# Score matmuls that read 32 rows of keys and queries a head instead of 17

## The chip, the cores and the metric

The kernel runs on one core of a Trainium2 chip, in one launch. The metric is the device time of that core in microseconds; lower is better. A core has a matrix engine (TensorE, in the profile PE for its matmuls and PEld for its weight loads), a vector engine (VectorE, DVE), an engine for functions such as exp and tanh (ScalarE, ACT), a general one (GpSimd, POOL), and queues for transfers to and from memory. They run side by side and wait for each other through semaphores.

## The reference

Four layers in a row on `x` of shape (1, 2048, 512): attention, feed-forward, attention, feed-forward, each on a normalized copy of `x` and added to it. Both attentions use the same weights, and so do both feed-forwards. Cut to what matters:

```python
def _A_ref(x, wqkv, wo):
    B, S, D = x.shape
    H = 32; Dh = D // H                      # 32 heads of 16
    qkv = (x @ wqkv).reshape(B, S, 3, H, Dh).transpose(2, 0, 3, 1, 4)
    q, k, v = qkv[0], qkv[1], qkv[2]
    scores = jnp.einsum("bhqd,bhkd->bhqk", q, k) * Dh ** -0.5
    p = softmax(scores, axis=-1)
    o = jnp.einsum("bhqk,bhkd->bhqd", p, v)
    return o.transpose(0, 2, 1, 3).reshape(B, S, D) @ wo

def _B_ref(x, w1, w2):                       # w1 (512, 1792), w2 (1792, 512)
    return silu(x @ w1) @ w2

x = x + _A_ref(layernorm(x), A_wqkv, A_wo)
x = x + _B_ref(layernorm(x), B_w1, B_w2)
x = x + _A_ref(layernorm(x), A_wqkv, A_wo)
x = x + _B_ref(layernorm(x), B_w1, B_w2)
```

## The kernel before

**Tiling.** The sequence of 2048 tokens is cut into 4 chunks of 512 queries and 16 tiles of 128 keys, the 32 heads into 8 head blocks of 4. Keys and queries lie transposed, with a head's elements along the partitions: `KT` holds for each head block 128 partitions by 2048 keys, `QT` 128 partitions by 512 queries. Head j of a block has partitions 32j to 32j+31. The first 16 of these hold the head's elements. Row 16 holds a bias: in `KT` it is one (added from `onescol`, L242), in `QT` it is minus the largest absolute key times the absolute query, summed over the head (made with `Bm`, L322), so that the exponentials need no maximum over the scores. Rows 17 to 31 hold zeros, in both: the padded weights `wk_pad` and `wq_pad` are cleared and filled in 16 of 32 columns, and `onescol` and `Bm` are zero there. All 128 partitions of `KT` and `QT` are written by single instructions, L242 and L327.

**A unit.** The attention stage of a layer is a loop over units (chunk, head block, key tile), 4 x 8 x 16 = 512 a layer, 1024 in all. For one unit:
- `emit_s` (L520) makes four score matmuls, one for each head of the block. The weights are 128 keys of the head, the moving data its 512 queries, and the sum runs over the head's rows, `VS` = 17 of them. Each pair of heads shares a PSUM tile `s_ps` of 2 x 512; there are three such tiles.
- ScalarE takes the exponential of each pair (L585, 1024 elements a partition) into `p_sb`.
- `emit_pv` (L532) makes four value matmuls with 128 rows, which add to `o_ps` over all 16 key tiles. Their weights `vd` hold one head's 16 value columns and a column of ones in a field of 128 columns that is otherwise zero, so that the four heads land on different partitions of one result. GpSimd fills them (L141).

The scores of the next unit are issued before the values of this one, and the values of the second pair wait for the next unit.

**Order.** The order on TensorE, ScalarE and VectorE is as the program is written (`manual_schedule`). Other work is cut into small steps and pumped into the units: keys and queries of the next head blocks (L225, L298, L322), the heads' output at the end of a block (`oT` L573, then a transpose L336 and a scaling L343), and, while chunk c is in attention, the output projection, layer norm and feed-forward of chunk c-1 (L362, L371, L194, L392, L429, L399), in layer 0 also the next layer's values (L269). The pump spreads the steps that are left over the units that are left (`todo`). A step that waits for VectorE stops TensorE's stream, with the scores behind it.

**Boundaries.** At the end of a head block (key tile 15 to key tile 0) the last values must be summed, `o_ps` is copied, and the copy is transposed before TensorE goes on. At the start of chunks 1 to 3 the projection and the layer norm of the chunk before come first in the pump, each a chain from TensorE to VectorE and back.

**Ends of the layers.** After the last unit of a layer the last chunk's projection, norm and feed-forward run without attention beside them, and after layer 0 also the next layer's values and first keys.

Of the kernel before, what the change touches and what calls it, by code (L numbers as in the profile page):

```python
# [18 lines left out]
def kernel(  # L19
# [16 lines left out]
    P = 128  # L36
# [8 lines left out]
    SCALE = DH ** -0.5  # L45
    EPS = 1e-5
    VS = DH + 1
    NG = 4
    NR = 2

# [18 lines left out]
    def wide(name):  # L69
        return spool.tile([P, 2, 512], FP32, name=name, tag="s")  # L70
# [54 lines left out]
    KT = xpool.tile([P, HB, S], BF16, name="KT")  # L125
# [4 lines left out]
    for i in range(NR):  # L130
        vd = xpool.tile([P, NG, 4, P], BF16, name=f"vd{i}")
        nc.gpsimd.memset(vd[:], 0.0)
# [5 lines left out]
    def vd_fill(va, hb, g, slot):  # L138
        for j in range(4):
            h = 4 * hb + j  # L140
            nc.gpsimd.tensor_copy(  # L141
                out=vdq[slot][:, :, j, 32 * j : 32 * j + DH],
                in_=va[:, NG * g : NG * (g + 1), DH * h : DH * (h + 1)],
            )
# [372 lines left out]
    def emit_s(QT, hb, kt):  # L517
        tiles = [wide("s_ps") for _ in range(2)]
        for j in range(4):
            nc.tensor.matmul(  # L520
                tiles[j // 2][:, j % 2, :],
                lhsT=KT[32 * j : 32 * j + VS, hb, kt * P : (kt + 1) * P],
                rhs=QT[32 * j : 32 * j + VS, :],
                start=True,
                stop=True,
            )
        return tiles

    def emit_pv(o_ps, p_sb, kt, pr):
        for jj in range(2):  # L530
            j = 2 * pr + jj
            nc.tensor.matmul(  # L532
                o_ps[:, :],
                lhsT=vdq[kt // NG % NR][:, kt % NG, j, :],
                rhs=p_sb[:, jj, :],
# [14 lines left out]
    for L in range(2):  # L550
# [15 lines left out]
        o_ps = None  # L566
        pend = []
        s_now = emit_s(QTs[0][0], 0, 0)
        left = 0

# [5 lines left out]
        for u, (c, hb, kt) in enumerate(units):  # L576
# [16 lines left out]
            if u + 1 < len(units):  # L593
                nc_, nhb, nkt = units[u + 1]
                s_now = emit_s(QTs[nc_][nhb], nhb, nkt)
# [32 lines left out]

            if kt % NG == 0 and u > 0 and u + NG * (NR - 1) < len(units):
                _, fhb, fkt = units[u + NG * (NR - 1)]  # L630
                vd_fill(va, fhb, fkt // NG, fkt // NG % NR)

# [51 lines left out]
```

## Time and profile before

| | |
|---|---|
| time, median of 3 runs | 2186.79 us (2185.69 to 2189.19) |
| span of the profiled execution | 2190.4 us |
| mean granted clock of TensorE in it | 0.968 |
| exponentials, L585 | 2048 of 1237 ns |
| score matmuls, L520 | 4096 of 385 ns |
| value matmuls, L532 | 4096, of which 3909 are recorded, of 386 ns |
| head block in layer 0, chunk 0 | 29.60 us, most of them |
| first head block of chunks 1, 2, 3 in layer 0 | 43.78, 43.78, 43.76 us |

The span runs from the first to the last instruction of the one execution that was profiled; it lies 3.6 us above the median of the runs. The head blocks are counted from the start of a block's first exponential to that of the next block's. Durations of matmuls overlap, since matmuls are pipelined, so that busy times of TensorE say how long something was in its pipe, not how much it did. The clock row is the share of TensorE's full clock that was granted; in this trace it is either full or half at any instant, and a digit of the row is a mean over a slice of 55 us. In the lists of groups a row has the line, the engine and the operation, what is written and read, the shapes and the count, then the busy time, the mean time of one, and the idle time before with what ended it. In the timeline a row has the start, the length, the engine, the line, the operation and the count of instructions that follow each other.

### The profile page before, as it was taken

Reading aid. Unit: us, or ns where it says so; the run is one execution under the profiler, and the core shown is the slowest. Engines: PE = TensorE matmul, PEld = TensorE weight load, DVE = VectorE, ACT = ScalarE, POOL = GpSimd, SP = SyncE. Lnnn points to the kernel's source line nnn. Section 1 sums busy time; section 2 is a strip of 40 time slices with the busy share of each in tenths; the row PEclk is TensorE's granted clock in tenths of the full one; section 3 lists DMA queues with packets and bytes.
Section 4 is the critical chain, followed back from the end, with each engine's and each line's share of the span. In section 5 each row is a group of like instructions: output and inputs, shape, how many; then the busy total and the mean of one; then the engine's idle time right before and its main releaser. Section 6 shows DMA issues by size and latency. Waiting matters only on the chain.

```text
span 2190.4 us, 28490 instructions
## 1 busy us (share of the span) xinstructions
PE 1952.9 (89%) x10355; PEld 717.0 (33%) x10561; DVE 558.6 (26%) x1106; ACT 1943.4 (89%) x2152; POOL 248.2 (11%) x1055
## 2 busy tenths in 40 slices
PE   3999988999889998899778999998999989998996
PEld 1333323333333333333222333333333333333332
DVE  6323212112311133112343323131113111131114
ACT  0899989999799997999517999999999999999981
POOL 3111101111011110111000111111111111111100
PEclk9999999999899998999878999999999999999997
DMA  4000000000000000000000000000000000000000
GB/s 144 1 1 1 1 1 1 1 1 1 1 1 1 1 1 1 1 1 1 1 0 1 1 1 1 1 1 1 3 8 1 1 1 8 4 1 1 6 5 10
DMA packets 8477, 11.79 MB, mean 5 GB/s; under 512 B 400, under 2 KB 7312, under 8 KB 8336
## 3 DMA queue, kind: packets, MB, share of 16 engines
q1 hardware_dynamic: 7280, 8.39, 1.1%
q8 instruction: 82, 1.34, 0.3%
q10 hardware_dynamic: 1056, 1.57, 0.2%
q14 instruction: 59, 0.48, 0.1%
HBM read 7.86 MB, written 2.10 MB: 5 GB/s over the span
## 4 chain that ended last, share of the span: by engine, by line
PE 64%; ACT 21%; issue 8%; DVE 6%; DMA 0%; ACTq 0%; DVEq 0%
PE o_ps L532 30%; ACT p_sb L585 19%; PE s_ps L520 17%; PE y_ps L399 3%; PE k_ps L225 3%; PE q_ps L298 3%; PE h_ps L392 2%; PE y_ps L371 2%; PE v_ps L269 2%; ACT t_sb L429 1%; DVE st L149 1%; PE t_ps L194 1%; DVE oT L573 1%; PE at_ps L336 1%; DVE hT L477 1%
## 5 line engine op out<-in xcount | busy, mean ns | idle before, releaser
L585 ACT ACTIVATE p_sb<-s_ps 128x1024 bf16<-128x1024 f32 x2048 | 1920.4, 1237 | 123.3 <-PE s_ps L520 123.3
L532 PE MATMUL o_ps<-p_sb,vd 128*128 128x512 bf16 x3909 | 1045.1, 386 | 19.7 <-issue 15.5
L520 PE MATMUL s_ps<-QT,KT 17*128 17x512 bf16 x4096 | 575.3, 385 | 89.6 <-ACT p_sb L585 85.3
L532 PEld LDWEIGHTS <-vd 128*128 128x128 bf16 x4096 | 318.8, 98 | 484.8 <-issue 246.8
L141 POOL COPY vd<-v 128x64 bf16<-128x64 bf16 x1024 | 231.5, 239 | 1868.1 <-PE o_ps L532 1723.6
L520 PEld LDWEIGHTS <-KT 17*128 17x128 bf16 x4096 | 175.1, 91 | 591.1 <-issue 571.2
L573 DVE CAST oT<-o_ps 128x512 bf16<-128x512 f32 x64 | 44.3, 692 | 380.3 <-PE o_ps L532 380.3
L430 DVE SCALAR_TENSOR_TENSOR hT<-t_sb,h_ps 128x512 bf16<-128x512 f32 x84 | 57.5, 684 | 301.5 <-ACT t_sb L429 301.5
L399 PE MATMUL y_ps<-w_sb,hT 128*128 128x512 bf16 x445 | 128.0, 388 | 5.4 <-DVE hT L477 4.5
L392 PE MATMUL h_ps<-xnT,w_sb 128*128 128x512 bf16 x438 | 126.6, 387 | 3.2 <-DVE hT L477 1.4
L313 DVE CAST qc<-q_ps 128x512 bf16<-128x512 f32 x64 | 44.2, 691 | 173.0 <-PE q_ps L298 173.0
L242 DVE TENSOR_SCALAR KT<-k_ps,onescol 128x512 bf16<-128x512 f32 x56 | 42.0, 750 | 172.1 <-PE k_ps L225 172.1
L194 PE MATMUL t_ps<-ident,xn 128*128 128x128 bf16 x256 | 32.2, 271 | 57.1 <-DVE xn L182 55.4
L405 DVE SCALAR_TENSOR_TENSOR x_sb<-y_ps,x_sb 128x512 bf16<-128x512 f32 x32 | 22.1, 690 | 232.7 <-PE y_ps L399 232.7
L476 ACT ACTIVATE t_sb<-h_ps 128x1024 f32<-128x1024 f32 x14 | 14.3, 1024 | 75.1 <-PE h_ps L392 59.0
L298 PE MATMUL q_ps<-xnT,wq_pad 128*128 128x512 bf16 x255 | 77.0, 385 | 2.5 <-DVE attn L343 2.4
L225 PE MATMUL k_ps<-xnT,wk_pad 128*128 128x512 bf16 x254 | 78.7, 402 | 0.3 <-issue 0.2
L429 ACT ACTIVATE t_sb<-h_ps 128x512 f32<-128x512 f32 x84 | 76.9, 916 | 0.0
L399 PEld LDWEIGHTS <-hT 128*128 128x128 bf16 x448 | 44.3, 100 | 61.4 <-issue 6.1
L392 PEld LDWEIGHTS <-w_sb 128*128 128x128 bf16 x448 | 44.7, 100 | 58.4 <-issue 8.3
L327 DVE CAST QT<-q_ps 128x512 bf16<-128x512 f32 x64 | 44.2, 691 | 37.0 <-PE q_ps L322 37.0
L371 PE MATMUL y_ps<-wo_sb,aT 128*128 128x512 bf16 x126 | 40.8, 425 | 7.5 <-DVE aT L366 7.3
(58 smaller groups left out, 572.8 us busy)
## 6 DMA issues: line engine op xcount, KB each, us to landing
w_sb<-in_B_w_dram SPq DMA_DIRECT2D x2, 1792.0 KB, 15.0
x_sb<-in_A_x_dram SPq DMA_DIRECT2D x4, 512.0 KB, 9.8
out_dram<-x_sb SPq DMA_DIRECT2D x16, 128.0 KB, 1.7
wraw<-in_A_wqkv_dram ACTq DMA_DIRECT2D x1, 1024.0 KB, 7.6
wv_sb<-in_A_wqkv_dram ACTq DMA_DIRECT2D x1, 512.0 KB, 10.0
wo_sb<-in_A_wo_dram SPq DMA_DIRECT2D x1, 512.0 KB, 12.3
```

What stands on the lines that cost most here:

```text
L141: nc.gpsimd.tensor_copy(out=vdq[slot][:, :, j, 32 * j : 32 * j + DH], in_=va[:, NG * g : NG * (g + 1), DH * h : DH * (h + 1)],)
L225: nc.tensor.matmul(ps, lhsT=wk_pad[:, ct, 4 * hb : 4 * hb + 4, :].rearrange("p h s -> p (h s)"), rhs=xnT[:, ct, :], start=(ct == 0), stop= ...
L298: nc.tensor.matmul(cell["ps"][:, :], lhsT=wq_pad[:, ct, 4 * hb : 4 * hb + 4, :].rearrange("p h s -> p (h s)"), rhs=xnTs[c][:, ct, :], star ...
L371: nc.tensor.matmul(cell["ps"][:, :], lhsT=cell["aT"][:, ct, :], rhs=wo_sb[:, ct, :], start=(ct == 0), stop=(ct == CT - 1),)
L392: nc.tensor.matmul(ps, lhsT=w1_sb[:, ct, ft * P : (ft + 1) * P], rhs=xfT[:, ct, :], start=(ct == 0), stop=(ct == CT - 1),)
L399: nc.tensor.matmul(ps, lhsT=hT[:, ft, tq * P : (tq + 1) * P], rhs=w2_sb[:, ft, :], start=(ft == 0), stop=(ft == FT - 1),)
L429: nc.scalar.activation(t_sb[:, 0, :], hc["ps"][:, :], ACT.Tanh, scale=0.5)
L430: nc.vector.scalar_tensor_tensor(out=cell["hT"][:, ft, :], in0=t_sb[:, 0, :], scalar=1.0, in1=hc["ps"][:, :], op0=ALU.add, op1=ALU.mult,)
L520: nc.tensor.matmul(tiles[j // 2][:, j % 2, :], lhsT=KT[32 * j : 32 * j + VS, hb, kt * P : (kt + 1) * P], rhs=QT[32 * j : 32 * j + VS, :], ...
L532: nc.tensor.matmul(o_ps[:, :], lhsT=vdq[kt // NG % NR][:, kt % NG, j, :], rhs=p_sb[:, jj, :], start=(kt == 0 and j == 0), stop=(kt == TT - ...
L573: nc.vector.tensor_copy(out=oT[:], in_=o_ps[:])
L585: nc.scalar.activation(p_sb[:].rearrange("p a b -> p (a b)"), s_now[pr][:].rearrange("p a b -> p (a b)"), ACT.Exp, scale=float(SCALE),)
```

## The change

A constant `KR` = 32 takes the place of `VS` = 17 in the slices of both operands of the score matmuls. A score matmul then sums over the 32 partitions that belong to its head. The 15 rows added hold zeros in both operands, so that the sums are the same. No tile, loop, or order is changed.

```diff
@@ -45,6 +45,7 @@
     SCALE = DH ** -0.5
     EPS = 1e-5
     VS = DH + 1
+    KR = 32
     NG = 4
     NR = 2
 
@@ -519,8 +520,8 @@
         for j in range(4):
             nc.tensor.matmul(
                 tiles[j // 2][:, j % 2, :],
-                lhsT=KT[32 * j : 32 * j + VS, hb, kt * P : (kt + 1) * P],
-                rhs=QT[32 * j : 32 * j + VS, :],
+                lhsT=KT[32 * j : 32 * j + KR, hb, kt * P : (kt + 1) * P],
+                rhs=QT[32 * j : 32 * j + KR, :],
                 start=True,
                 stop=True,
             )
```

## The prediction

> **What bounds the kernel now.** I read the page's busy times first, then its costliest groups, then the clock row, and then the timeline and the clock of single stretches.
>
> ```profile
> PE 1952.9 (89%) x10355; PEld 717.0 (33%) x10561; DVE 558.6 (26%) x1106; ACT 1943.4 (89%) x2152; POOL 248.2 (11%) x1055
> PEclk9999999999899998999878999999999999999997
> ...
> L585 ACT ACTIVATE p_sb<-s_ps 128x1024 bf16<-128x1024 f32 x2048 | 1920.4, 1237 | 123.3 <-PE s_ps L520 123.3
> L532 PE MATMUL o_ps<-p_sb,vd 128*128 128x512 bf16 x3909 | 1045.1, 386 | 19.7 <-issue 15.5
> L520 PE MATMUL s_ps<-QT,KT 17*128 17x512 bf16 x4096 | 575.3, 385 | 89.6 <-ACT p_sb L585 85.3
> L532 PEld LDWEIGHTS <-vd 128*128 128x128 bf16 x4096 | 318.8, 98 | 484.8 <-issue 246.8
> L520 PEld LDWEIGHTS <-KT 17*128 17x128 bf16 x4096 | 175.1, 91 | 591.1 <-issue 571.2
> ```
>
> Attention is 1024 units (2 layers, 4 chunks, 8 head blocks, 16 key tiles). Each gives ScalarE two exponentials and TensorE four score and four value matmuls plus some pumped work. The start times of the exponentials in the trace put most units 1.81 us apart, and 687 of the 1023 steps from one unit to the next are under 1.82 us: there ScalarE sets the pace (it works without a gap) and TensorE has room. The other 336 steps are longer; they are paced by TensorE's chain, and there alone can a change on TensorE move the end. The clock row shows why some of them are long: it dips inside the attention stage. The same place of two successive head blocks, TensorE alone:
>
> ```profile
> 1195.59 0.40 PE L336 MATMUL at_ps<-ident,oT 128*128 128x128 bf16 x4 [0.79 <-DVE oT L573]
> 1195.92 0.40 PE L520 MATMUL s_ps<-QT,KT 17*128 17x512 bf16 x4
> 1196.25 2.73 PE L532 MATMUL o_ps<-p_sb,vd 128*128 128x512 bf16 x6
> 1198.77 1.06 PE L225 MATMUL k_ps<-xnT,wk_pad 128*128 128x512 bf16 x2
> 1199.76 0.40 PE L520 MATMUL s_ps<-QT,KT 17*128 17x512 bf16 x4
> ```
>
> ```profile
> 1226.87 0.40 PE L336 MATMUL at_ps<-ident,oT 128*128 128x128 bf16 x4 [0.79 <-DVE oT L573]
> 1227.20 0.39 PE L520 MATMUL s_ps<-QT,KT 17*128 17x512 bf16 x4
> 1227.53 1.47 PE L532 MATMUL o_ps<-p_sb,vd 128*128 128x512 bf16 x6
> 1228.83 0.59 PE L225 MATMUL k_ps<-xnT,wk_pad 128*128 128x512 bf16 x2
> 1229.36 0.39 PE L520 MATMUL s_ps<-QT,KT 17*128 17x512 bf16 x4
> ```
>
> From score group to score group the first takes 3.84 us, the second 2.16: the same matmuls, at half clock in the first. **A drop at such a block boundary costs 1.68 us.**
>
> **When the clock drops.** The trace's clock record changes only at instants that are whole multiples of 3.413 us apart, so I cut the span along that grid. Six cells of it (stretch, length, busy time of PE, PEld, DVE, ACT, POOL, then the granted clock):
>
> ```profile
> 1192.88:1196.30 3.42, 2.48 (x18) 0.71 (x17) 0.95 (x2) 3.42 (x5) 0.91 (x4) 1.00 0.00 0
> 1196.30:1199.71 3.41, 3.41 (x12) 0.98 (x8) 0.42 (x1) 2.11 (x3) 0.00 (x0) 0.50 0.03 5
> 1493.26:1496.67 3.41, 2.39 (x15) 0.72 (x13) 1.29 (x2) 3.41 (x6) 0.83 (x4) 1.00 0.02 5
> 1223.60:1227.02 3.42, 2.48 (x15) 0.76 (x14) 0.69 (x1) 3.42 (x5) 0.91 (x4) 1.00 0.00 0
> 1947.19:1950.60 3.41, 2.39 (x14) 0.74 (x12) 1.28 (x2) 3.41 (x5) 0.90 (x4) 1.00 0.00 0
> 1070.00:1073.42 3.42, 1.83 (x10) 0.61 (x8) 0.88 (x2) 1.37 (x2) 0.92 (x4) 1.00 0.00 0
> ```
>
> After the first and the third cell the clock halves; after the last three it does not. So busy time is not what decides: 2.48 us of it dropped and 1.83 us was kept. The cell at 1070 holds no score matmul; the cell at 1192.88 holds eight. I therefore weigh each matmul by the rows it uses: a 512-column matmul streams for some 213 ns at full clock (value matmuls start 216 ns apart in the trace), a transpose for a quarter of that, and a score matmul counts 17/128 of its 213 ns. Missing matmul records are put back from their weight loads, which are all there. The cell at 1192.88 holds 828 ns of full matmuls, 213 of transposes and 1707 of score matmuls: (828 + 213 + 1707 x 17/128) / 3413 = 0.371. At 1493.26 it is 0.351, at 1947.19 0.378, at 1070.00 0.397, at 1223.60 0.447. **Over all full-clock cells from the start of attention on, every one of the 16 that drop lies at 0.371 or less and every other at 0.378 or more.** Were a score matmul counted as 32 rows, as a whole row group, 1192.88 would be at 0.430 and have dropped while 1070.00 at 0.397 was kept: the order breaks. Moving the grid's edge by 50 ns leaves it clean for weights of 12 to 24 rows and not for 32. This is an inference from one trace: nothing in it shows the counter itself.
>
> The Trainium skill, "TensorE: Matmul & The Clock Gate", section "HAM oscillation — how this bites in real kernels", says that idle gaps over about 3.4 us send the clock back. It speaks against this change, since no row count enters. By it the sum would be nothing, as against my 12 us. The cells above, busy for 2.4 of 3.4 us before a drop, don't agree with it, so I go by them.
>
> **The change part by part.** No instruction is added, removed or moved, no queue passed, no wait added: the producers of KT and QT (L242, L327) write all 128 partitions already. What changes is the rows of 4096 weight loads and 4096 matmuls, 17 to 32.
>
> Own time of the matmuls: 385 ns with 17 rows, 386 with 128 rows, so 0 to 1 ns; I take 0. Weight loads: 91 ns with 17 rows, 98 with 128 rows, so +0 to +7 ns; 32 rows is nearer to 17 and I take 0. What hides it is TensorE's slack in the 687 units at ScalarE's pace; without it the price is the second rival's.
>
> Clock: each score matmul now counts 32/128. A cell of attention holds some 1707 ns of them, so it gains 1707 x 15/128 / 3413 = 0.059. Nine drops lie inside attention:
> 1. Block boundaries (slow from 127.9, 1196.3, 1496.7 us): 0.324, 0.371 and 0.351 become 0.383, 0.430 and 0.409, all above 0.378. Slid over every position of the grid, these dips fall under 0.375 at 13 to 28% of positions now, and at no more than 2% with 32 rows. They go: 3 drops. At 1.68, 1.64 (31.24 against 29.60 us for the head block) and 1.4 us that is 4.7 us.
> 2. First dip of chunks 1 to 3 in layer 0 (slow 308.8 to 315.7, 564.8 to 571.7, 820.8 to 827.7). From 0.371, 0.367, 0.362 to 0.400, 0.396, 0.392: kept at this position, but the first saving moves everything against the grid, and over all positions half still drop (52%; 61% before). Price: TensorE is busy 5.50 of 6.83 us at half clock, so up to 2.75; with the waits on VectorE between, 2.5. Three times 2.5, half of it: 3.8 us; between 0 and 7.5.
> 3. Second dip of those chunks (slow 336.1 to 343.0, 592.1 to 599.0, 848.1 to 855.0), where TensorE waits over 2 us for the layer norm: 0.267 to 0.281 and the like, so it drops at 71 to 74% of positions. Price: score groups 2.8 us apart for two units where 1.83 is usual, some 2 us. The second slow cell may not come: cells at half clock rose at 0.77 to 0.80 and stayed at 0.74 to 0.77, and with 32 rows the first slow cell here goes from 0.76 to 0.82. Now 3 x 2 = 6 us; after, 3 x 0.72 x 1.2 = 2.6. Gain 3.4; between 0 and 6.
>
> The drops at the ends of the layers (1076 to 1169, after 2135 us) hold hardly any score matmuls and stay; their position against the grid can shift by one cell, about 1.7 us either way.
>
> Sum: 4.7 + 3.8 + 3.4 = 11.9 us. The profiled execution took 2190.4 us, so 2178.5 for it; it lies 3.6 us above the median of the runs (2186.79, from 2185.69 to 2189.19), as a different number of drops would make it. Against the median: **2175 us**. Own range of this case: gains of 4.7 (only part 1) to 18.2 (all nine), 2168.6 to 2182.1, and 4 us more to either side for the position of the grid.
>
> **Rivals.**
> *Rows don't count, or zero rows don't, or a whole row group always did.* Then nothing moves: 2187, within the spread of the runs. For it: the rule above, and that the order broken by 32 rows rests on two cells, by 0.033 of a cell (113 ns). Against: 16 drops split without error at 17. And the value matmuls' weights are mostly zeros (vd fills 17 of 128 columns), yet they must be counted in full: at a weight of 0.75 the split has 7 errors.
> *Wider reads cost time on TensorE's chain.* Place: the weight loads of L520 in units that TensorE paces. Price: up to 7 ns for each of four loads in 336 units, 9.4 us: 2196. It decides if loads lengthen by over 4 ns (336 x 4 x 3.3 ns is 4.4 us, 0.2%) and no drop goes. For it: a group's first load starts only 4 ns ahead of its first matmul. Against: four score matmuls start within 120 ns of each other when their buffers are free, with loads of 90 ns, so loads overlap; and the 128-row load is only 7 ns longer.
> *Dips move to worse positions.* All six chunk dips drop already, so they can only get fewer; this caps the loss at the layer ends, some 3 us, against 4.7 us saved: 2185.
>
> **How the numbers follow.** A measurement of this kernel can tell 0.2% (4.4 us) from no change. Forecast, with dips moving to worse positions as its weak end: 0.74, of which 0.70 is over 4.4 us faster and 0.04 within. Rows that don't count: 0.12, of which 0.11 within and 0.01 noise to the slow side. Costlier reads: 0.14, slower. So faster 0.70, same 0.15, slower 0.15. The range is 2163 (all nine gone, 4 us more) to 2191 (no change, upper end); what is left out is most of the costlier reads and a little below.
>
> **What would show it.** Right: the granted clock full at the boundaries that dropped; the mean clock up from 0.968 to about 0.975; score loads still near 91 ns; the chunk blocks of layer 0 at 38 to 42 us where they take 43.78. Wrong: drops after cells whose share, counted with 32 rows, is well over 0.378; as many drops at block boundaries as before; loads near 98 ns and steps of over 1.83 us in plain units.

## The result, and the profile after

| | before | after |
|---|---|---|
| time, median of 5 runs | 2186.79 us (2185.69 to 2191.04) | 2174.37 us (2172.95 to 2177.73) |
| ratio, with its 95% interval | | 0.9941 [0.9926, 0.9957] |
| span of the profiled execution | 2190.4 us | 2171.7 us |
| mean granted clock in it | 0.968 | 0.979 |

The change saved 12.4 us by the medians; 11.9 were forecast. The busy times, the clock row and the costliest groups of the changed kernel (lines have moved by one):

```profile
PE 1934.3 (89%) x10355; PEld 712.9 (33%) x10561; DVE 558.7 (26%) x1106; ACT 1942.9 (89%) x2152; POOL 247.7 (11%) x1055
PEclk9999999999999999999789999999999999999997
...
L586 ACT ACTIVATE p_sb<-s_ps 128x1024 bf16<-128x1024 f32 x2048 | 1921.3, 1249 | 105.2 <-PE s_ps L521 105.2
L533 PE MATMUL o_ps<-p_sb,vd 128*128 128x512 bf16 x3909 | 1034.4, 383 | 19.6 <-issue 15.3
L521 PE MATMUL s_ps<-QT,KT 32*128 32x512 bf16 x4096 | 574.5, 383 | 89.9 <-ACT p_sb L586 85.7
L533 PEld LDWEIGHTS <-vd 128*128 128x128 bf16 x4096 | 317.7, 98 | 478.6 <-issue 237.4
L521 PEld LDWEIGHTS <-KT 32*128 32x128 bf16 x4096 | 175.2, 90 | 589.8 <-issue 569.1
```

Counts are the same; a score matmul takes 383 ns where it took 385, its weight load 90 where it took 91. What changed is the clock row: the 8s inside attention are gone, the dip between the layers is left. ScalarE's wait for scores fell from 123.3 to 105.2 us.

The block boundary whose counterpart cost 3.84 us before, in TensorE's timeline:

```profile
1180.83 0.40 PE L337 MATMUL at_ps<-ident,oT 128*128 128x128 bf16 x4 [0.79 <-DVE oT L574]
1181.16 0.39 PE L521 MATMUL s_ps<-QT,KT 32*128 32x512 bf16 x4
1181.49 1.47 PE L533 MATMUL o_ps<-p_sb,vd 128*128 128x512 bf16 x6
1182.80 0.59 PE L226 MATMUL k_ps<-xnT,wk_pad 128*128 128x512 bf16 x2
1183.32 0.39 PE L521 MATMUL s_ps<-QT,KT 32*128 32x512 bf16 x4
```

Score group to score group it is 2.16 us: the same matmuls at full clock. Cells of the 3.413 us grid of the changed kernel (stretch, length, busy time of PE, PEld, DVE, ACT, POOL, granted clock):

```profile
1539.63:1543.04 3.41, 2.39 (x15) 0.82 (x14) 1.29 (x2) 3.41 (x6) 0.61 (x3) 1.00 0.00 0
1543.04:1546.46 3.42, 3.26 (x24) 1.38 (x24) 0.68 (x2) 3.42 (x5) 0.00 (x0) 1.00 0.00 0
327.89:331.31 3.42, 1.36 (x6) 0.40 (x5) 2.93 (x16) 2.74 (x3) 0.00 (x0) 1.00 0.00 0
331.31:334.72 3.41, 2.97 (x15) 1.41 (x16) 1.12 (x4) 1.94 (x2) 0.43 (x2) 0.50 0.02 5
334.72:338.13 3.41, 3.41 (x27) 1.57 (x27) 1.37 (x4) 2.89 (x4) 0.45 (x3) 1.00 0.02 5
```

The first cell is a twin of the one at 1493.26 us before: 2.39 us of PE busy, 0.284 (before) and 0.285 (after) of the cell in full rows, 0.500 in score matmuls. With 17 rows its share was 0.284 + 0.500 x 17/128 = 0.351, and the clock halved; with 32 rows it is 0.285 + 0.500 x 32/128 = 0.410, and the clock stayed. The next three are the second dip of chunk 1 (the layer norm): it still drops, at 0.281, but one cell is slow where there were two.

By head blocks, the 18.7 us between the two profiled spans split into:
- three block boundaries, 31.24 to 29.60, 31.28 to 29.60 and 32.67 to 31.29 us: 4.7 us;
- three chunk starts of layer 0, 43.78, 43.78, 43.76 to 40.04, 40.10, 40.21 us: 11.0 us. Of the six dips there, three still drop, each for one cell;
- the start and the ends of the layers: the 3 us that are left, where nothing was changed; the position of the grid would do it, which two traces can't show.

These two executions lie further apart than the medians. The time of an execution is 1.8 us more than its span (2173.48 us against 2171.7), so the profiled one of before took about 2192.2 us, 5.4 above its median; that of after lies 0.9 below its own. 18.7 less 5.4 and 0.9 is 12.4.

### The profile page after: what moved, and what is told of

It is laid out like the page before. It is cut to its first block, busy times and chain, and to the rows that moved or that the text cites. A ratio compares the mean times of both kernels' runs of the same rounds, so it can differ in the third digit from the quotient of the medians.

```text
span 2171.7 us, 28490 instructions
## 1 busy us (share of the span) xinstructions
PE 1934.3 (89%) x10355; PEld 712.9 (33%) x10561; DVE 558.7 (26%) x1106; ACT 1942.9 (89%) x2152; POOL 247.7 (11%) x1055
## 4 chain that ended last, share of the span: by engine, by line
PE 62%; ACT 22%; issue 9%; DVE 6%; DMA 0%; ACTq 0%; DVEq 0%
PE o_ps L533 29%; ACT p_sb L586 20%; PE s_ps L521 16%; PE y_ps L400 3%; PE k_ps L226 3%; PE q_ps L299 2%; PE h_ps L393 2%; PE y_ps L372 2%; PE v_ps L270 2%; ACT t_sb L430 1%; DVE st L150 1%; PE t_ps L195 1%; DVE oT L574 1%; PE at_ps L337 1%; DVE hT L478 1%
## 5 line engine op out<-in xcount | busy, mean ns | idle before, releaser
L586 ACT ACTIVATE p_sb<-s_ps 128x1024 bf16<-128x1024 f32 x2048 | 1921.3, 1249 | 105.2 <-PE s_ps L521 105.2
L533 PE MATMUL o_ps<-p_sb,vd 128*128 128x512 bf16 x3909 | 1034.4, 383 | 19.6 <-issue 15.3
L521 PE MATMUL s_ps<-QT,KT 32*128 32x512 bf16 x4096 | 574.5, 383 | 89.9 <-ACT p_sb L586 85.7
L521 PEld LDWEIGHTS <-KT 32*128 32x128 bf16 x4096 | 175.2, 90 | 589.8 <-issue 569.1
## 6 DMA issues: line engine op xcount, KB each, us to landing
wo_sb<-in_A_wo_dram SPq DMA_DIRECT2D x1, 512.0 KB, 12.4
```

The lines of the kernel that those rows point to most:

```text
L521: nc.tensor.matmul(tiles[j // 2][:, j % 2, :], lhsT=KT[32 * j : 32 * j + KR, hb, kt * P : (kt + 1) * P], rhs=QT[32 * j : 32 * j + KR, :], ...
L533: nc.tensor.matmul(o_ps[:, :], lhsT=vdq[kt // NG % NR][:, kt % NG, j, :], rhs=p_sb[:, jj, :], start=(kt == 0 and j == 0), stop=(kt == TT - ...
L586: nc.scalar.activation(p_sb[:].rearrange("p a b -> p (a b)"), s_now[pr][:].rearrange("p a b -> p (a b)"), ACT.Exp, scale=float(SCALE),)
```

## The experiments

The theory: after a cell of 3.413 us in which the columns streamed, each weighted by its rows of 128, come to under 3/8 of the cell, TensorE runs at half clock. Rivals: the clock goes by busy time alone; a row group counts whole; a wider read is itself better for the stream; the gain is luck of the grid's position.

### The rule by itself (e1)

A kernel that only runs phases of back-to-back matmuls on TensorE:

```diff
+    for r in (96, 64, 56, 52, 48, 44, 40, 32, 17):
+        rows(r, 128)          # 128 matmuls of r rows x 512 columns
+        warm()                # 96 of 128 rows
+    # zeros in both operands; 32 weight columns
+    for r in (32, 17, 8):
+        for _ in range(128):
+            for j in range(4):
+                rows(r, 1, 32 * j, j)   # four row groups, four banks
```

> A kernel of its own that measures the clock rule: it copies x to the output and leaves the whole layers out. TensorE alone runs phases of 128 back-to-back 512-column matmuls (no wait inside) with 96, 64, 56, 52, 48, 44, 40, 32 and 17 rows, each followed by 96 matmuls of 128 rows; then 128 rows of zeros in both operands; then 128 rows with 32 weight columns; then four heads side by side, as the score matmuls stand, with 32, 17 and 8 rows each. Theory (the clock halves after a cell of 3.413 us whose row-weighted share is under 3/8; zeros count): phases of 52 rows and more keep the full clock, 48 rows (0.371) is at the edge, 44 and fewer fall to half within two cells although TensorE never pauses; zeros keep the full clock; four times 32 and four times 17 keep it, four times 8 (0.25) loses it. Rival 'busy time decides': every phase keeps the full clock. Rival 'a row group of 32 counts whole': 40 to 56 rows count as 64 and keep the clock, 32 and 17 both count 0.25 and lose it, four times 8 keeps it.

The groups by shape (the second number after the bar is the mean time of one matmul in ns):

```profile
L50 PE MATMUL ps<-xin 40*128 40x512 bf16 x128 | 49.5, 581 | 0.0
L50 PE MATMUL ps<-xin 44*128 44x512 bf16 x128 | 49.1, 577 | 0.0
L50 PE MATMUL ps<-xin 48*128 48x512 bf16 x128 | 48.6, 573 | 0.0
...
L66 PE MATMUL ps<-xin 128*32 128x512 bf16 x128 | 27.8, 379 | 0.0
L50 PE MATMUL ps<-xin 56*128 56x512 bf16 x128 | 27.8, 376 | 0.0
L50 PE MATMUL ps<-xin 52*128 52x512 bf16 x128 | 27.8, 376 | 0.0
...
L63 PE MATMUL ps<-zer 128*128 128x512 bf16 x125 | 27.6, 379 | 0.2
```

And four stretches of the same kernel (length, busy time of PE, PEld, DVE, POOL, granted clock): 52 rows, 48 rows in their first microseconds, 48 rows on the way down, 48 rows after.

```profile
178.00:205.90 27.90, 27.80 (x129) 12.06 (x130) 0.00 (x0) 0.00 (x0) 1.00 0.00 1
226.70:230.00 3.30, 3.30 (x16) 1.41 (x15) 0.00 (x0) 0.00 (x0) 1.00 0.00 0
230.00:233.00 3.00, 3.00 (x15) 1.32 (x14) 0.00 (x0) 0.00 (x0) 0.98 0.00 0
233.20:275.00 41.80, 41.80 (x99) 14.34 (x97) 0.00 (x0) 0.00 (x0) 0.50 0.00 0
```

TensorE is busy without a gap in the last three, and but for 0.1 us in the first. 52 rows hold the full clock for the whole phase; 48 rows, a share of 0.371 at 216 ns a matmul (52 rows: 0.401), lose it after the first cell that they fill, and then the same 128 matmuls take 48.6 us where they took 27.8. 44, 40, 32 and 17 rows lose it too. Zeros hold it, and so do 32 weight columns: neither the data nor the columns of weights count. Four groups side by side hold it with 32 and with 17 rows each (0.53) and lose it with 8 (0.25). Each of the rivals on the clock fails here: busy time, since all phases are busy; whole row groups, since 40 to 48 rows fall and 52 hold within the same two groups.

### A quarter of the change, at the boundaries (e2), and the other three quarters (e3)

```diff
     def emit_s(QT, hb, kt):
         tiles = [wide("s_ps") for _ in range(2)]
+        KR = 32 if kt < 4 else VS      # e2;  e3: VS if kt < 4 else 32
```

> 32 rows only in the score matmuls of key tiles 0 to 3 of each head block (a quarter of them, those around the boundary), 17 in the rest. Theory: no drop at block boundaries, at most two in each chunk start of layer 0, as with 32 rows everywhere; 2172 to 2180 us. Rival 'a 32-row matmul is itself better for the stream': a quarter of the gain, about 2184. Rival 'luck of the grid': drops at boundaries as before, 2183 to 2191.

> The complement: 32 rows in key tiles 4 to 15, 17 rows in key tiles 0 to 3. Theory: the cells that drop are those with the boundary in them, so boundary drops come as before the change (about 7 over 42 dips by the share of grid positions, 3 in the profile of before), and the first dips of the chunks too; the second dips of the chunks, which hold tiles above 3, may release a cell earlier; 2181 to 2189 us. Rival 'a 32-row matmul is itself better': three quarters of the gain, about 2178. Rival 'luck of the grid': anything from 2174 to 2191, without boundary drops being tied to the edge tiles.

| | time | ratio to before |
|---|---|---|
| e2, key tiles 0 to 3 with 32 rows | 2176.51 us | 0.9947 [0.9928, 0.9966] |
| e3, key tiles 4 to 15 with 32 rows | 2190.1 us | 1.0017 [1.0006, 1.0028] |

A quarter of the wider reads gives the gain of all of them, within the intervals; three quarters give none. In the trace of e2 no block boundary drops; in that of e3 eight do, at 127.5, 410.8, 601.9, 919.4, 1192.4, 1492.8, 1946.8 and 2042.3 us. One of them, the cell before and the slow cell:

```profile
407.40:410.80 3.40, 2.23 (x13) 0.66 (x12) 1.29 (x2) 3.40 (x6) 0.87 (x4) 0.99 0.00 0
410.80:414.20 3.40, 3.40 (x15) 1.36 (x14) 0.56 (x2) 2.14 (x3) 0.00 (x0) 0.50 0.00 0
```

So the gain is tied to the cells with the boundary in them. A gain from the reads themselves would be shared out as 1 to 3, and luck would not follow the key tiles. e3 is 1.1 us beyond what was expected. By the head blocks its eight boundary drops cost 11.6 us, 1.4 to 1.7 each; the sliding had given about seven. Its chunk starts (41.31, 39.94 and 41.16 us) are shorter than the 43.8 us of before, so the other three quarters may well help there, as was expected of the second dips; in this trace the boundaries take it back. Why e3 lies a little above the kernel before is not shown.

### Other work in the boundary's cell, 17 rows (e4)

```diff
+    def warm(n):
+        dm = narrow("dm")
+        for _ in range(n):
+            nc.tensor.matmul(dm[:, :], lhsT=wo_sb[:, 0, 0:P], rhs=wo_sb[:, 1, :],
+                             start=True, stop=True)
     def heads_piece(oT, hb, attn):
         def a():
+            warm(3)
```

> 17 rows as before, but three spare full matmuls (their result is not used) ahead of the transposes at each end of a head block, where TensorE waits for the copy of the sums: 640 ns more of full rows in each boundary cell, a share of 0.19 more. Theory: no drop at block boundaries and none at the first dips of the chunks; the second dips stay; 2172 to 2179 us if the spare work fits in the wait. Rivals that look for the gain in the reads themselves, or in no more than luck: 2187 or more, since work is added.

2200.32 us, ratio 1.0056 [1.0037, 1.0075]: a miss in time, though the clock rose to 0.976. In chunk 0 the theory held: after the first two blocks all took 29.6 us, in both layers, none dropped, and the spare work cost nothing. In chunks 1 to 3 the blocks of 31.29 us rose to 32.00 us, and most of the others grew too, by 0.3 to 0.8 us. The same block end there, first with the spare work, then in the changed kernel without it:

```profile
1464.70 1.47 PE L541 MATMUL o_ps<-p_sb,vd 128*128 128x512 bf16 x5
1466.01 0.81 PE L336 MATMUL dm<-wo_sb 128*128 128x512 bf16 x3
1466.87 0.38 PE L345 MATMUL at_ps<-ident,oT 128*128 128x128 bf16 x4
```

```profile
1448.66 1.47 PE L533 MATMUL o_ps<-p_sb,vd 128*128 128x512 bf16 x6
1449.96 0.39 PE L337 MATMUL at_ps<-ident,oT 128*128 128x128 bf16 x4
```

In chunks 1 to 3 a begun step and the next values stand ahead of the transposes, so these don't wait for VectorE even without the spare work (the second timeline), and the 0.64 us go straight onto TensorE's chain. Two boundaries, at 600.1 and 634.2 us, dropped all the same. Between the profiles of before and e4 the first blocks of chunks 1 to 3 in layer 0 won 11.5 us (43.8 each before; 39.80, 38.84 and 41.14 us), and the other blocks of chunks 1 to 3 lost some 24. Zero rows in matmuls that run anyway cost nothing that the profile shows (383 ns a matmul, 385 before); spare matmuls are free here only inside a wait.

### Between and below: 24 rows (e5), 1 row (e6)

```diff
-    KR = 32
+    KR = 24          # e5;  e6: 1
```

> 24 rows in every score matmul. Theory (row-weighted share): sliding the grid over the profile of before with a weight of 24/128, about 1 boundary drop is left of 7, and the chunk dips are as with 32 rows: 2173 to 2181 us. Rival 'only a full row group of 32 changes anything': no change, 2185 to 2191.

> 1 row in every score matmul; 15 of 16 elements of a head and the bias row are left out of the scores, all else is computed. Theory: with a weight near 0 the same sliding gives about 13 boundary drops instead of 7, and longer cells at the chunk starts: 2193 to 2210 us, mean clock 0.955 to 0.963, with score matmuls and loads of the same 385 and 91 ns. Rival 'fewer rows are cheaper or equal': 2187 or less.

| rows | 1 | 17 | 24 | 32 |
|---|---|---|---|---|
| time, us | 2198.03 | 2186.93 | 2177.77 | 2174.37 |
| ratio to before | 1.0063 [1.0040, 1.0085] | | 0.9961 [0.9949, 0.9974] | 0.9941 [0.9926, 0.9957] |

The time falls with the rows at every step (the last column is from the runs of the result). 24 rows, short of a full row group, give most of the gain, and one row loses 11 us, with a score matmul at 387 ns and a load at 91. In the trace of e6, 12 block boundaries drop, in that of e5 none. Reading less costs more here, and not through the reads.

### A version that beats both (e7 to e11)

The drops that are left after the change come after cells with few score matmuls to widen, or none: the layer norms at the chunk starts and the ends of the layers. There the spare matmuls of e4 fit, since TensorE waits.

```diff
+    def fill(n):               # n matmuls of 128 rows x 512 columns, result not used
...
         def tr(tq):
+            if at_end["on"]:
+                fill(24 if tq == 0 else 0 if wide_ps else 2)
+            elif tq == 0:
+                fill(at_end["ln"])          # 7 in layer 0, at both norms of a chunk
             transpose_tile(...)
...
     def heads_piece: fill(3 if at_end["on"] else at_end["first"] if hb == HB - 1 else 0)
     epilogue: fill(3), fill(2); v_piece: fill(2); q_piece bias: fill(14)   # at the ends
     ffn_last: fill(6) ahead of the second matmuls
```

> 32 rows, and in layer 0 spare full matmuls at the two dips of the chunk starts that are left: 3 ahead of the transposes at the end of a chunk's last head block, 7 ahead of the first transpose of the layer norm. Theory: no drop left in the chunk starts, their head blocks go from 40.1 to about 38.5 us, 3 to 6 us in all: 2168 to 2172 us. If the spare work is on TensorE's chain, as at the boundaries of chunks 1 to 3 in the run with 17 rows, up to 3 x 2.1 us are given back: 2174 to 2177.

> The same, and spare full matmuls in TensorE's waits at the end of each layer and at the start of layer 1: 24 ahead of a layer norm's first transpose, 2 to 6 ahead of the projections, transposes and second feed-forward matmuls, 14 ahead of the bias matmul. Theory: the half-clock cells at the ends, 78 us of the 100 in the profile of after, go or shrink, and the matmuls in them take half the time: 10 to 18 us, 2154 to 2164. If spare work delays real work, since these stretches are one chain between TensorE and VectorE, less, up to a loss: 2165 to 2180.

> 32 rows and spare matmuls at the ends of the layers and the start of layer 1 alone, none at the chunk starts. Theory: the chunk starts are as in the changed kernel (half-clock cells in each, head blocks of some 40 us), the ends are as with all spare work: 2158 to 2163 us, level with the run that had both, since the spare work at the chunk starts gave back what it won.

> The same, and the 7 spare matmuls ahead of the first transpose of the layer norm in the chunk starts of layer 0, but not the 3 at the chunk's last head block, whose block grew from 29.7 to 31.1 us. Theory: the second dips are gone, about half of the first dips drop for one cell: 2155 to 2160 us. If those 7 delay the transposes: 2161 to 2165.

> 17 rows, as before the change, with the spare matmuls at the ends of the layers alone. Theory (the two gains lie at different places and add): boundary and chunk drops as before the change, ends without: 12 to 15 us under before, 2172 to 2176. Rival 'any work that warms the clock gives the same gain': level with the run with 32 rows, 2158 to 2163.

| | time | ratio to before | clock in the trace |
|---|---|---|---|
| e7: 32 rows, chunk starts (3 and 7) | 2175.5 us | 0.9944 [0.9932, 0.9956] | 0.981 |
| e8: the same and the ends | 2160.7 us | 0.9882 [0.9868, 0.9896] | 0.997 |
| e9: 32 rows, ends alone | 2162.1 us | 0.9886 [0.9869, 0.9902] | 0.992 |
| e10: 32 rows, ends and 7 at the layer norm | 2159.03 us | 0.9871 [0.9851, 0.9890] | 0.995 |
| e11: 17 rows, ends alone | 2175.58 us | 0.9944 [0.9928, 0.9959] | 0.984 to 0.986 in its runs |

e7 cleared the chunk starts (no drop left there, 38.8 us a block) and won nothing, where 3 to 6 us were expected: the last head block of chunks 1 and 2 grew by 1.4 us (29.71 to 31.14). What takes it back are seven more spare matmuls there. The norm of the next layer is pumped into that block, by the same code as the norm at the chunk start, and so gets its 7 too. In e7:

```profile
522.36 1.04 PE L551 MATMUL o_ps<-p_sb,vd 128*128 128x512 bf16 x4
523.23 1.67 PE L146 MATMUL dm<-wo_sb 128*128 128x512 bf16 x7
524.96 0.38 PE L204 MATMUL t_ps<-ident,xn 128*128 128x128 bf16 x4
```

The changed kernel has no wait at this place (its transposes start at 524.17 us, 0.95 after the value matmuls, here 2.60), so the 7 go onto TensorE's chain. The expectation for e10 puts the loss down to the 3 matmuls at the end of the chunk's last head block; that was wrong, since e10 leaves these out and its blocks still take 31.14 us, while e9, without the 7, has 29.71. The ends are worth 12 us, and they add to the rows: 17 rows with the ends filled lie 13.5 us above 32 rows with the ends filled. e9 lies 1.4 us above e8, within what these runs tell, and e10 is the lowest; its interval overlaps those of e8 and e9, so that the 7 at the layer norms are not shown to pay by themselves. 7 at the chunk start's norm alone, without the seven that cost 1.4 us, were not run. The end of layer 0 in e8's timeline:

```profile
1069.48 1.04 PE L389 MATMUL y_ps<-wo_sb,aT 128*128 128x512 bf16 x4
1070.35 5.34 PE L146 MATMUL dm<-wo_sb 128*128 128x512 bf16 x24
1077.34 0.72 PE L204 MATMUL t_ps<-ident,xn 128*128 128x128 bf16 x8 [1.64 <-DVE xn L192]
```

The 24 spare matmuls end 1.64 us before the normalized tile arrives, and the real matmuls around them run at full clock: four output matmuls in 1.04 us, where the changed kernel has, at the same place:

```profile
1072.66 1.89 PE L372 MATMUL y_ps<-wo_sb,aT 128*128 128x512 bf16 x4 [0.52 <-DVE aT L367]
1081.37 1.04 PE L195 MATMUL t_ps<-ident,xn 128*128 128x128 bf16 x8 [6.82 <-DVE xn L183]
```

## Why the prediction was right

**Own time of the matmuls and loads, taken as 0.** Right: 383 and 90 ns with 32 rows, 383 and 91 with 24, 387 and 91 with 1. The rival of costlier reads falls: e5 and the change, with more rows, are faster, in order of rows.

**The share and its edge.** Right. It was read from one trace as an order of cells, 0.371 against 0.378; e1 shows it with TensorE never pausing, 0.371 against 0.401. In the trace of after, cells counted with 32 rows split at 0.361 and 0.375 without error; counted with 17, cells that kept the clock lie down to 0.347, below one that lost it at 0.361. The traces of e4 and e6, counted like this, have cells out of order, by up to 0.023. Counted once more over the eleven traces of the whole kernel (before, after, e2 to e10), with every matmul taken to stream from 55 ns after its recorded start, 122 of the 123 cells that lost the clock lie at 0.372 or less (one, in e4, at 0.379), and all 6412 that kept it at 0.375 or more. The 55 ns are fitted; without them 11 cells are out of place. So 3/8 of a cell is the edge, as far as these traces can tell. The prediction's step of 50 ns holds one way alone: with the grid's edge 50 ns earlier the order stays, with it 50 ns later two cells are out of order at 17 rows. Its 0.324 for the cell before 127.9 us is read too low; with the value matmul whose record is missing put where its weight load stands (127.65 us) it is some 0.36, which is still under the edge.

The grid itself is in the Trainium skill, "TensorE: Matmul & The Clock Gate", section "What's actually happening", as a free-running window of 3413 ns; every change of the clock in these traces is a multiple of that apart. The same page's rule on idle gaps, which by itself gave a gain of nothing, is not the whole of it: in e1 the clock halves with no gap at all.

**Part 1, block boundaries, 4.7 us.** Right in the profiled pair: three drops gone, 4.7 us by the head blocks. e2 and e3 tie them to the tiles at the boundary.

**Parts 2 and 3, chunk starts, 3.8 + 3.4 = 7.2 us.** The mechanism was right, the size too small, though within the bounds given (0 to 13.5 together): 11.0 us in the profiled pair, since three of six dips dropped where 3.7 were expected and every one of them lasted one cell. The weaker ground, the earlier rise of the second dip, came out: all cells at the second dips that dropped rose after one.

**The ends, not in the sum.** They were to stay slow and to shift by some 1.7 us either way. They stayed slow, and e8 and e9 show by what filling them is worth; the start and the ends together are 3 us shorter in the profiled pair.

**Rows that don't count.** Falls with e1, e5 and e6. **Dips that move to worse positions** did not occur in the profiled pair: the chunk dips only got fewer.

**The number: in part luck.** 11.9 us were forecast and 12.4 came, but the two don't measure the same thing. The parts were priced from one profiled execution, in which all six chunk dips dropped, and the sum was then taken off the median of the runs. That execution lies 5.4 us above the median by time (the prediction had 3.6, since it set the span beside the times). In the profiled pair the gain was 18.7 us, 6.8 more than the sum (3.8 of it at the chunk starts, 3 at the start and the ends): the prediction's own figure for the profiled execution was 2178.5 us, and the span after is 2171.7. The sum was 6.8 us short, the two profiled executions lay 6.3 us further apart than the medians, and the two nearly cancel. What is shown is the mechanism, the direction and the size within some 7 us. The lower end of the range, 2163, is also not what its working gives: 2168.6 less 4 is 2164.6.

## What to carry to other kernels

Cut the trace along the grid on which the clock changes and count matmul columns weighted by rows, not busy time: here a cell under 3/8 (0.375) paid with a slow cell after it, 1.4 to 1.7 us at each block boundary. Matmuls that use few rows starve this count; here zero rows raised it for nothing (383 ns a matmul, 385 before), and spare matmuls raised it where TensorE waited, but cost about their full time where it did not (e4: 0.71 us for three; e7: 1.4 us for seven).

## What the runs showed of the hardware

- A TensorE that never pauses lost half its clock with matmuls of 48, 44, 40, 32 and 17 rows of 128 (one at a time, 512 columns); at 52 rows and more it kept it.
- The data didn't matter: 128 rows of zeros held the clock as real data did (27.6 us for 125 recorded matmuls), and 32 columns of weights as well as 128 (27.8 us for 128).
- The way back has the same edge, as far as the traces can tell. In the eleven traces of the whole kernel, with the same 55 ns, half-clock cells with up to 0.754 of what half the clock can stream stayed at half, and cells from 0.739 up rose; 0.75 of half the clock is 3/8 of the full one.
- The spread between runs of one kernel goes with the mean clock: 18 runs of the kernel before, beside e2 to e4, went from 2178.38 us at 0.976 to 2192.75 us at 0.966. That the position of the grid makes the difference fits the rule, but only one of its executions was traced.
- The three chunk starts of the kernel before were 256.0 us apart, which is 75 cells of the grid, so that all three met it in the same position, a bad one (0.371, 0.367 and 0.362 before the first dips). A kernel with a period can keep such a position from one repeat to the next.
